# Six dummy products ahead of x's transposition and two behind it, in place of five and one

## The chip, the cores and the metric

The kernel runs on one core of a Trainium2 chip. The metric is device time in microseconds for one launch. A profile is one execution recorded instruction by instruction; its span runs from the first recorded instruction to the last, and the device time of the same execution is somewhat longer.

## The reference

Two blocks read the same x (2048 tokens by 448) and a gate mixes them. Block A is attention with 16 heads of 28 in four segments of 512 tokens, each causal within itself, with a memory carried from segment to segment. Block B is a layer norm and then a two-layer network over the token axis.

```python
x = A_x                                              # (1, 2048, 448), bf16
g = sigmoid((x * gate_w).sum(-1, keepdims=True))
# A: q, k, v = x @ wq, x @ wk, x @ wv; for each segment s of 512 tokens
p = softmax(qs @ ks.T * scale + mask); a_dot = p @ vs
a_mem = (phi(qs) @ M) / (phi(qs) @ z + 1e-6)
o = sigmoid(beta) * a_mem + (1 - sigmoid(beta)) * a_dot
M = M + phi(ks).T @ vs; z = z + phi(ks).sum(0)
a = concat(o) @ wo
# B
u = gelu(einsum('bsd,sf->bdf', layernorm(x), w1) + b1)
b = (einsum('bdf,fs->bds', u, w2) + b2).transpose(0, 2, 1)
return g * a + (1 - g) * b
```

The products that the change touches are no part of this: they multiply a constant by itself, and nobody reads what they write.

## The kernel before

The order of all work is written out by hand in one string, `PLAN` (L30 to L114). An item such as `trx.0.2@P1` names a helper, its arguments, the engine (P for PE, A for ACT, D for DVE, G for POOL, S for SP) and sometimes a bank or buffer number. L1077 walks through the items in order and each helper records one or several operations. Each engine executes its own operations in the order of the string. `Sched.op` (L156) works out from the resources that an operation reads and writes which others it must wait for, and `emit_engine` (L239) puts those waits, as semaphore waits, ahead of the instruction. Between two PE operations that write the same PSUM bank no wait is made (L187).

At the start the string has, on PE: `warm`, then eight `trx` pieces with two transposes each, then `fill`, then the products `kc` of x with the k weights.

- `warm` (L470, matmuls at L474) issues `NWARM` products of a constant array of ones, 128 rows by 512 columns, into PSUM bank 3. `NWARM` is 5 (L25). It reads nothing that is loaded and waits for nothing but the start of the program.
- `ldx` (L375) loads x; the first two pieces, two tiles of 128 tokens each, go into `x0`, with the DMA itself issued at L361 on SP. `xw` (L540) copies 64 columns on ACT so that the last slice is 128 wide.
- `trx` (L544, matmul at L552) transposes 128x128 pieces of the first 512 tokens on PE, against an identity that POOL makes at L465. It waits for the load of x. The other 1536 tokens come transposed by DMA (`xtd`, L417).
- `ex` (L559) copies the transposed pieces from PSUM to `xTb`, on DVE or ACT through the helper `copy` (DVE at L371, ACT at L369).
- `fill` is the helper `keep` (L480, matmul at L481): one product of the same constants into bank 3.
- `pad` (L573) spreads the loaded weights to 32 columns for each head, on DVE at L371. `kc` (L614, matmul at L618) waits for the copies of `ex` and for the padded k weights. `qf` and `kf` follow at L608, and `l2`, `l` at L627.
- `ldwv` (L392) loads wv, `wvc` (L396) copies half of its last slice on DVE.

Behind this stand the value products (L694, L706), the scores (L838) with exponentials on ACT (L848), the products with the probabilities (L879), and the two large products of the token network (`mm_u` at L994, `mm_y` at L1047). Those parts are the same in both kernels.

Of the kernel before, what the change touches and what calls it, by code (L numbers as in the profile page):

```python
# [21 lines left out]
NO = 3  # L22
NTA = 3
RING = 4096
NWARM = 5  # L25
GELU_BATCHES = ((0, 7), (7, 14))


# [117 lines left out]
class Sched:  # L146
# [9 lines left out]
    def op(self, eng, fn, reads=(), writes=(), name=None, dma=False, group=None, out=False):  # L156
        if dma:
            if group is None:
                self._dma_uid += 1
                evspace = "dma_u%d" % self._dma_uid  # L160
            else:
                evspace = "dmag_" + group
        else:
            evspace = eng
        o = Op(eng, evspace, fn, name, len(self.ops))
        if out:
            self.out_spaces.add(evspace)
        deps = {}

        def need(d):  # L170
            if d is o or (dma and d.evspace == evspace):
                return
            key = d.evspace
            old = deps.get(key)
            if old is None or old.idx < d.idx:
                deps[key] = d

        for r in reads:
            if r.last_write is not None:
                need(r.last_write)  # L180
            if r.psum and eng != "PE":
                for rd in r.reads:
                    if rd.eng != eng and rd.eng != "PE":
                        need(rd)
        for r in writes:
            w = r.last_write
            if w is not None and not (r.psum and eng == "PE" and w.evspace == "PE"):  # L187
                need(w)
            for rd in r.reads:
                if not (r.psum and eng == "PE" and rd.evspace == "PE"):  # L190
                    need(rd)
        o.deps = list(deps.values())
        for d in o.deps:
            d.is_event = True
        if dma:
            o.is_event = True
        for r in reads:
            r.reads.append(o)
        for r in writes:
            r.last_write = o  # L200
            r.reads = []
        self.ops.append(o)
        self.per_eng[eng].append(o)
        return o
# [43 lines left out]
def build_kernel(nc, X, WQ, WK, WV, WO, BETA, W1, B1, W2, B2, GW, OUT):  # L248
    sch = Sched(nc)
    op = sch.op  # L250
# [13 lines left out]
    def R(name, n=None, psum=False):  # L264
        if n is None:
            return Res(name, psum)
        return [Res(f"{name}{i}", psum) for i in range(n)]
# [5 lines left out]
    R_bank = R("psum", 8, psum=True)  # L273

    def bank(b):
        return ps[:, b, :]
# [25 lines left out]
    ones = nc.const_aps.tensor(1.0, [128, 512], BF16)  # L302
# [167 lines left out]
    def warm(eng, u):  # L470
        def fn(e):
            last = None
            for _ in range(NWARM):
                last = e.matmul(bank(3)[:, 0:512], ones[:, 0:128], ones[:, 0:512], start=True, stop=True,  # L474
# [3 lines left out]
        op("PE", fn, reads=[], writes=[R_bank[3]])  # L478

    def keep(eng, u):  # L480
        op("PE", lambda e: e.matmul(bank(3)[:, 0:512], ones[:, 0:128], ones[:, 0:512], start=True, stop=True,  # L481
                                    skip_group_check=True), reads=[], writes=[R_bank[3]])

    def acttab(eng, u):
        op("ACT", lambda e: e.activation(gth[:, 0:1], ones[:, 0:1], ACT.Exp), reads=[], writes=[R_gth[0]])
# [577 lines left out]
    def st(eng, u, T):  # L1063
        i = slot["out", T]
        for c0, n in [(0, D)] if T < NT - 1 else [(0, 224), (224, 224)]:
            dma(eng, out2[T * 128 : T * 128 + 128, c0 : c0 + n], outst[:, i, c0 : c0 + n],
                reads=[R_outst[i] if c0 == 0 else R_out2], final=True)

    emit_op = dict(ldx=ldx, ldwk=ldwk, ldwq=ldwq, ldwv=ldwv, wvc=wvc, ldgw=ldgw, ldsm=ldsm, ldwo=ldwo, xtd=xtd, xtc=xtc, ldr=ldr, dve0=dve0,
                   id=ident_, mz=mz, oz=oz, warm=warm, fill=keep, acttab=acttab, btg=btg, btr=btr, gcp=gcp, b1c=b1c_, b2c=b2c_, tb=tb,  # L1070
                   bet=bet, xw=xw, trx=trx, ex=ex, pad=pad, rid=rid, kc=kc, kf=kf, qf=qf, l=l, l2=l2, l3=l3, gw=gw, gr=gr,
                   ek=ek, eq=eq, vf=vf, vl=vl, vl2=vl2, ev=ev, gt=gt, gc=gc, pkm=pkm, pke=pke, pkn=pkn, pqm=pqm,
# [61 lines left out]
```

## Time and profile before

| | before |
|---|---|
| four runs | 175.59, 176.68, 176.68, 177.79 us |
| median | 176.68 us |
| the profiled execution: device time | 175.59 us |
| the profiled execution: span | 173.8 us |
| PE busy | 167.3 us in 1286 matmuls |
| dummies of L474 | 5, starting at 0.82 us, 631 ns each in the median |
| dummy of L481 | 1, starting at 4.72 us, 380 ns |
| transposes of L552 | 16, starting at 3.48 us, 226 ns each in the median |

A line of the timeline gives the start in us, the time from the first start to the last end, engine, line, operation, what is written and read with the shapes, and how many; in brackets the idle time ahead of it and what ended it. [...]matmuls overlap: the rate is read from the distance between two starts, not from the duration. In the table by stretches a row gives the stretch, its length, PE's busy time with the number of matmuls, the clock granted as the records have it, the share of the DMA engines, and GB/s. A line of the chain of waits gives a start, a length and the work or the transfer that the end waited for. The profiled execution is the lowest of the four runs; it lies 1.09 us below the median.

### The profile page before, as it was taken

What the parts mean: (1) busy time and instruction counts of PE and PEld (TensorE: products, weight loads), DVE (VectorE), ACT (ScalarE), POOL (GpSimd) and SP (SyncE); (2) the same over time, 40 slices, a digit from 0 to 9 for tenths busy, and PEclk for the clock granted to TensorE, in tenths of its full rate; (3) what the DMA queues carried; (4) which work ended last, traced back from release to release, by engine and by line L of the source; (5) the groups of instructions that cost most, each with busy time, mean ns of one, the idle gap of its engine ahead of it and who ended that gap; (6) DMA issues with size and microseconds to landing.
All of it is one profiled execution on the core that took longest, in us unless ns stands there. A gap on an engine that the chain in (4) does not pass through costs nothing.

```text
span 173.8 us, 3285 instructions
## 1 busy us (share of the span) xinstructions
PE 167.3 (96%) x1286; PEld 78.6 (45%) x1302; DVE 133.4 (77%) x276; ACT 121.1 (70%) x113; POOL 54.3 (31%) x100
## 2 busy tenths in 40 slices
PE   7799999999999999999999999999999999999994
PEld 3324334344534445444454446444444444455563
DVE  4789999868667875899599486899999879995113
ACT  4229899797969788878997979986697774600300
POOL 7045437880083055412200019033108242200000
PEclk9999999999999999999999999999999999999999
DMA  4897999335940495199690623500727268291022
GB/s 128 264 194 151 279 340 196 63 65 123 301 111 6 55 264 73 25 247 235 180 241 6 178 65 90 155 0 20 215 63 209 83 185 222 68 260 34 0 70 62
DMA packets 49456, 24.01 MB, mean 138 GB/s; under 512 B 14337, under 2 KB 49441, under 8 KB 49441
## 3 DMA queue, kind: packets, MB, share of 16 engines
q1 hardware_dynamic: 49441, 23.81, 55.3%
q8 instruction: 10, 0.16, 0.4%
q14 instruction: 5, 0.04, 0.1%
HBM read 18.48 MB, written 2.18 MB: 119 GB/s over the span
## 4 chain that ended last, share of the span: by engine, by line
PE 83%; DVE 9%; SPq 3%; DMA 2%; issue 1%
PE t L994 25%; PE t L1047 24%; PE t L608 7%; PE t L1020 7%; PE t L838 7%; PE t L879 5%; PE t L694 3%; DVE t L371 3%; SPq L361 3%; DMA t<-in_A_wv_dram 2%; PE t L627 2%; PE t L803 2%; DVE t L948 1%; PE t L706 1%; DVE t L1005 1%
## 5 line engine op out<-in xcount | busy, mean ns | idle before, releaser
L848 ACT ACTIVATE t<-t 128x2048 bf16<-128x2048 f32 x40 | 75.1, 1878 | 20.4 <-PE t L838 19.6
L861 POOL TENSOR_SCALAR_AFFINE_SELECT t<-t 128x1024 bf16<-128x1024 bf16 (+1 forms) x40 | 37.4, 954 | 82.2 <-ACT t L848 82.2
L994 PE MATMUL t<-t 128*128 128x448 bf16 x224 | 49.0, 353 | 0.3 <-issue 0.2
L1047 PE MATMUL t<-t 128*128 128x448 bf16 (+1 forms) x238 | 47.3, 342 | 0.2 <-issue 0.2
L1047 PEld LDWEIGHTS t<-t 128*128 128x128 bf16 x238 | 22.1, 98 | 19.5 <-issue 2.8
L994 PEld LDWEIGHTS t<-t 128*128 128x128 bf16 x224 | 20.9, 98 | 21.5 <-issue 2.5
L371 DVE CAST t<-t 128x512 bf16<-128x512 f32 (+1 forms) x23 | 15.3, 669 | 6.7 <-PE t L608 4.5
L369 ACT ACTIVATE t<-t 128x512 bf16<-128x512 f32 (+5 forms) x28 | 13.9, 533 | 8.8 <-PE t L627 6.1
L1056 DVE SCALAR_TENSOR_TENSOR t<-t 128x448 bf16<-128x448 f32 (+1 forms) x17 | 10.8, 648 | 11.3 <-PE t L1047 11.2
L608 PE MATMUL t<-t 128*128 128x512 bf16 x68 | 18.0, 381 | 0.7 <-issue 0.2
L838 PE MATMUL t<-t 28*128 28x512 bf16 (+3 forms) x256 | 15.9, 301 | 0.1
L1030 ACT ACTIVATE t<-t 128x448 bf16<-128x448 f32 x9 | 6.3, 722 | 12.0 <-PE t L1020 12.0
L1020 PE MATMUL t<-t 128*128 128x448 bf16 x64 | 14.2, 353 | 0.1
L1005 DVE TENSOR_SCALAR t<-t 128x448 bf16<-128x448 f32 x12 | 8.2, 682 | 5.8 <-PE t L994 5.7
L757 ACT ACTIVATE t<-t 128x1024 bf16<-128x1024 bf16 x12 | 12.6, 1050 | 0.0
L899 DVE STREAM_TRANSPOSE t<-t 128x512 f32<-128x512 f32 x16 | 11.1, 697 | 1.3 <-PE t L879 1.3
L940 DVE STREAM_TRANSPOSE t<-t 128x512 bf16<-128x512 bf16 x16 | 10.8, 687 | 0.1
L920 DVE SCALAR_TENSOR_TENSOR t<-t 128x448 bf16<-128x448 f32 x16 | 10.7, 686 | 0.1
L838 PEld LDWEIGHTS t<-t 28*128 28x128 bf16 x256 | 4.5, 92 | 13.9 <-issue 7.1
L694 PE MATMUL t<-t 128*128 128x449 bf16 x48 | 10.7, 355 | 0.0
L879 PE MATMUL t<-t 128*32 128x512 bf16 (+3 forms) x256 | 10.3, 301 | 0.0
L608 PEld LDWEIGHTS t<-t 128*128 128x128 bf16 x75 | 6.3, 97 | 8.5 <-issue 2.9
(77 smaller groups left out, 158.2 us busy)
## 6 DMA issues: line engine op xcount, KB each, us to landing
t<-in_B_w_dram SPq DMA_DIRECT2D x7, 1024.0 KB, 7.6
t<-in_B_w_dram SPq DMA_DIRECT2D x8, 896.0 KB, 5.4
out_dram<-t SPq DMA_DIRECT2D x15, 112.0 KB, 1.8
t<-in_A_x_dram SPq DMA_DIRECT2D x3, 448.0 KB, 7.0
t<-in_A_x_dram SPq DMA_DIRECT2D x2, 224.0 KB, 2.7
t<-in_A_wo_dram SPq DMA_DIRECT2D x4, 98.0 KB
t<-in_A_wk_dram SPq DMA_DIRECT2D x3, 112.0 KB, 3.3
t<-in_A_wq_dram SPq DMA_DIRECT2D x1, 336.0 KB, 3.5
```

The source lines that it names most:

```text
L369: op("ACT", lambda e: e.activation(out, in_, ACT.Copy), reads=reads, writes=writes)
L371: op(eng, lambda e: e.tensor_copy(out, in_), reads=reads, writes=writes)
L608: m = e.matmul(bank(b)[:, 0:512], wkq[:, c0 + c, 128 * hg : 128 * hg + 128], xTb[:, tc % NXT, c, :], start=first and c == 0, stop=last and ...
L694: m = e.matmul(bank(b)[:, 0 : D + 1], xTb[:, tc % NXT, c, k0 : k0 + 128], wvx[:, c, 0 : D + 1], start=tc == 0 and c == 0, stop=tc > 0 and ...
L757: op("ACT", lambda e: e.activation(et[:, i, :].rearrange("p (g t) -> p g t", g=2), two(T, hp, s), ACT.Exp), reads=[RT[2 * hp][s], RT[2 * h ...
L838: last = e.matmul(bank(hl)[:, c0 : c0 + w], kT[r, hg, s * 512 + j * 128 : s * 512 + j * 128 + 128], qT[r, hg, s * 512 + 128 * j : s * 512 ...
L848: op("ACT", lambda e: e.activation(punit(i).rearrange("p (a q) -> p a q", a=4), ps[:, 0:4, :], ACT.Exp, scale=SCALE), reads=R_bank[0:4], w ...
L861: op("POOL", lambda e: e.affine_select(d, d, pattern=pat, compare_op=ALU.is_ge, fill=0.0, base=0, channel_multiplier=-1), reads=[R_P[i]], ...
L879: last = e.matmul(bank(b)[32 * hl : 32 * hl + 32, 128 * j : 512], vaug[:, 4 * s + j, 32 * h : 32 * h + 32], p4[:, hl, c0 : c0 + w], start= ...
L994: op("PE", lambda e: e.matmul(bank(b)[:, 0:D], w[:, st, (ft % 2) * 128 : (ft % 2) * 128 + 128], xtile(st)[:, 0, :], start=(st == 0), stop= ...
L1020: last = e.matmul(bank(b)[:, 0:D], oT[:, hg, T * 128 : T * 128 + 128], wo_sb[:, hg, :], start=(hg == 0), stop=(hg == NHG - 1), skip_group_ ...
L1047: op("PE", lambda e, b=b, f=f, c0=c0, n=n: e.matmul(bank(b)[:, 0:n], w[:, f, c : c + 128], uT[:, f, c0 : c0 + n], start=(f == 0), stop=(f ...
```

## The change

The first group of dummies gets one more product, the later one gets a loop with a count of its own, set to 2. Operands, bank and order stay as they are.

```diff
-NWARM = 5
+NWARM = 6
+NFILL = 2
...
     def keep(eng, u):
-        op("PE", lambda e: e.matmul(bank(3)[:, 0:512], ones[:, 0:128], ones[:, 0:512], start=True, stop=True,
-                                    skip_group_check=True), reads=[], writes=[R_bank[3]])
+        def fn(e):
+            last = None
+            for _ in range(NFILL):
+                last = e.matmul(bank(3)[:, 0:512], ones[:, 0:128], ones[:, 0:512], start=True, stop=True,
+                                skip_group_check=True)
+            return last
+
+        op("PE", fn, reads=[], writes=[R_bank[3]])
```

## The prediction

> **What bounds the kernel now.** I read the page first, for the engine that fills the span, then the chain of waits, then the first ten microseconds, since the edit sits there.
>
> ```profile
> span 173.8 us, 3285 instructions
> ...
> PE 167.3 (96%) x1286; PEld 78.6 (45%) x1302; DVE 133.4 (77%) x276; ACT 121.1 (70%) x113; POOL 54.3 (31%) x100
> ...
> PEclk9999999999999999999999999999999999999999
> ...
> PE 83%; DVE 9%; SPq 3%; DMA 2%; issue 1%
> ```
>
> PE is busy for 96% of the span and carries 83% of the chain that ended last: what delays PE's stream in a stage without slack is paid at the end. The clock row is 9 in every slice, the first too; it says nothing of a slow start, so that has to be read from the spacing of the matmuls. The timeline of PE alone, and busy time in stretches that I cut at its events (the count takes in matmuls that straddle an edge):
>
> ```profile
> 0.82 2.29 PE L474 MATMUL t<-const-bfloat16-1.0 128*128 128x512 bf16 x5 [0.82 <-PEq L1119]
> 3.48 1.40 PE L552 MATMUL t<-t 128*128 128x128 bf16 x16 [0.37 <-DMA t<-in_A_x_dram]
> 4.72 0.38 PE L481 MATMUL t<-const-bfloat16-1.0 128*128 128x512 bf16 x1
> ```
> ```profile
> 2.95:3.48 0.53, 0.16 (x1) 1.00 1.07 370
> ...
> 5.10:5.99 0.89, 0.00 (x0) 1.00 1.00 342
> 5.99:10.06 4.07, 4.06 (x18) 1.00 0.97 217
> ```
>
> Record by record, the dummies of L474 start at 0.82, 1.20, 1.63, 2.05 and 2.48: 427 ns apart after the first. The first transposes of L552 are 107 ns apart; between 4.10 and 4.27 the step falls to 56 ns and stays there. The 18 products from 5.99 to 10.06 are 216 ns apart. So in this execution PE ran at half rate until about 4.22, 3.40 us after its first dummy. PE then stood still from about 5.1 to 5.99 for DVE's padding of the k weights. The chain of waits in the same stretch:
>
> ```profile
> 5.61 4.04 DMA t<-in_A_wv_dram
> ...
> 9.67 0.27 DVE t L371
> 9.95 0.23 DVE t L371
> 10.23 0.61 PE t L627 x4
> ```
>
> The chain does not run through PE before 10.23: it is SP issuing loads, the landing of wv, and two copies on DVE, for which PE waits 0.18 us after its 18 products. That 0.18 us is all the slack PE has there; beyond it, lateness goes into the chain.
>
> [...]
>
> **The change part by part.** The order of instructions differs on PE alone: 5 to 6 in the first group, 1 to 2 in the later one. No wait, DMA or buffer moves; bank 3 is written by PE before and after, so no semaphore is added.
>
> *Sixth dummy, its own cost.* It would start at 2.48 + 0.43 = 2.91 and stream until 3.33. x is there at 3.48, so 0.15 us of cover remain. Its record would end at 2.91 + 0.63 = 3.54, 0.06 past the first transpose, but dummies overlap by 0.20 (631 ns long, 427 apart), so I take 0, with 0.06 as upper end. Were x to land earlier than 3.33 the delay is bounded by 0.43. Queued behind it on PE: all 16 transposes, for which ACT and DVE wait.
>
> *Second product behind the transposes.* It starts at 4.72 + 0.22 = 4.93 and is over by 5.31; the next PE work starts at 5.99, released by DVE. Cover 0.68, cost 0. With PE still at half rate: the 16 transposes would end at 3.48 + 16 x 0.107 = 5.19, and two dummies at 5.19 + 2 x 0.427 = 6.05, up to 0.06 late plus the tail of a record, 0.2: 0 to 0.26, of which 0.18 is slack.
>
> *What the products do to the clock.* This does not appear as an edit, so I bound it. Between 0.82 and 4.22 the dummies streamed 5 x 0.427 = 2.13 us, 63% of 3.40; with the transposes (0.74) 84%. With six: 2.56 us, 75%, or 97%. [...] In an execution where 4.22 was missed, what is lost? [...] Each microsecond of cold PE after 5.99 costs (0.427 - 0.216)/0.427 = 0.49.
>
> That is the size of the scatter of the runs shown: 175.59, 176.68, 176.68, 177.79, steps of 1.1 on three values. The profiled execution (span 173.8, 1.8 around it) is the lowest, 1.09 under the median. If late clocks make the scatter, +1.09 is a change to full clock at 5.99 + (1.09 + 0.18)/0.49 = 8.6, +2.20 one at 10.8. No trace of such an execution is at hand: this is a reading, not a finding. In the profiled execution itself the gain is nothing, its clock being up before it matters.
>
> **Sum.** Against the profiled execution: 0 + 0 + 0.06 at most. Against the median: the ramp comes in time more often, -1.09, bounds -1.5 to 0, and a loss only through the covers named. Likeliest case: the median falls to the level of the profiled execution, 175.59 + 0.06, about **175.7**.
>
> **The rivals.**
>
> *Nothing changes* (176.7). [...] the scatter may come from the landing of wv or from the coarse steps of the timing. For it: the chain before 10.23 is DMA and DVE. Against: 0.18 us of slack is little, and PE is the bound ever after. Chance 0.28.
>
> *Slower: the dummies are themselves in the way* (177.2; 178.8 at worst). Place: PE's queue ahead of the first transpose and of the first k product. Decided when x lands before 3.33 or PE is cold at 5.19. Price 0.43 + 0.26 - 0.18 = 0.5 on the median, 177.2[...]. Against: covers of 0.15 and 0.68 us. Chance 0.16, of which 0.10 beyond 1%.
>
> *Faster than the profiled execution* (174.5). Eight cold transposes would go warm, 8 x 51 ns = 0.41, if the full clock came before 3.48, and DVE's first copy of the transposed x, released by PE at 4.47, would start earlier. Against: the chain then lies in wv's landing, and 0.4 shows up as 174.5 only by the 1.1 steps. Chance 0.12.
>
> That the products would not be issued, or be made one, is excluded by the order of instructions.
>
> **How the numbers follow.** Likeliest case 0.44, the rivals 0.28, 0.16, 0.12. A difference under 1% (1.8 us) is about what a measurement of this kernel can't tell from none. The likeliest case is by itself a gain of 0.6%; it exceeds 1% where the kernel before, timed beside it, stands at its 177.8 end, for which I give 0.18 of the 0.44. Faster: 0.18 + 0.12 = 0.30. Same: 0.26 + 0.28 + 0.06 = 0.60. Slower: 0.10. The range, 174.4 to 177.3, takes in the fast rival, the no-change case and the nearer slow one; it leaves out the 0.10 beyond 1%, and some 0.07 at the edges.
>
> **What would show it.** Right: six L474 records 427 ns apart, the first transpose still released by x's DMA at about 3.5, two records of the later dummy ending before DVE lets the first k product go at about 6.0, and 216 ns spacing from there on; a span of about 173.8, the whole gain lying in how often that span is met, so a narrower scatter. Wrong: a first transpose held by PE's own queue, k products 427 ns apart after 6.0, a span under 173.4, or the same three values with the same frequency.

## The result, and the profile after

| | before | after |
|---|---|---|
| runs beside each other | 56 | 35 |
| median | 176.96 us | 176.82 us |
| lowest and highest | 175.59, 178.22 | 176.04, 178.06 |
| profiled execution, span | 173.8 us | 175.0 us |

The ratio of after to before is 0.9996, 95% interval [0.9982, 1.0009]: no difference larger than 0.2%. The forecast was 175.7; the time lies in its range, but the gain of 0.6% did not come. The profiled execution of after is even 1.2 us longer than that of before, so the two profiles have to be read for what happens to differ between two executions, too.

The page of after, the same lines as before:

```profile
span 175.0 us, 3289 instructions
...
PE 167.7 (96%) x1288; PEld 78.6 (45%) x1304; DVE 133.1 (76%) x276; ACT 121.2 (69%) x113; POOL 54.1 (31%) x100
...
PE 80%; DVE 11%; SPq 4%; DMA 2%; issue 1%
```

Two matmuls more by count, PE busy 0.4 us longer, and 3% of the chain has gone from PE to DVE and SP. The timeline of PE in the opening of after (lines ahead of `keep` lie one further down than before, those behind it seven):

```profile
0.82 2.72 PE L475 MATMUL t<-const-bfloat16-1.0 128*128 128x512 bf16 x6 [0.82 <-PEq L1126]
...
3.60 1.25 PE L559 MATMUL t<-t 128*128 128x128 bf16 x16
4.68 0.60 PE L485 MATMUL t<-const-bfloat16-1.0 128*128 128x512 bf16 x2
5.90 2.77 PE L625 MATMUL t<-t 128*128 128x512 bf16 x12 [0.62 <-ACT t L370]
8.50 1.46 PE L615 MATMUL t<-t 128*128 128x512 bf16 x6
9.89 0.61 PE L634 MATMUL t<-t 64*128 64x512 bf16 x4
```

The sixth dummy ends at 3.54, the transposes begin at 3.60, the second product ends at 5.28, the k products begin at 5.90. The first transposes start at 3.60, 3.66 and 3.72, 67 and 55 ns apart where those of before are 107 apart until 4.20: PE was at its full rate by then, some 0.6 us earlier than in the profile of before. The last-slice products at L634 (L627 before) start at 9.89, 0.34 earlier than before. Only 0.09 of that is PE's own (its last k product starts at 9.58, before at 9.67). The rest comes from the load of wv, which lands at 9.21 here and at 9.64 before, and which the edit does not touch. The lead is gone at once. The chain of waits in after:

```profile
8.88 3.60 DMA t<-in_A_x_dram
12.47 0.02 issue
12.50 0.29 DVE t L372
```

The transposed second quarter of x lands at 12.47, DVE stands still for 0.53 us until then, and from there all is 0.2 us later than before. The other 1 us comes at 69 us, in code that neither edit touches. These are the waits of PE between 66 and 75 us in after (waiting, then released by whom, us in total, times, longest), and the stretches around it with PE, PEld, DVE, ACT and POOL busy, clock, DMA share and GB/s:

```profile
PE t L810 <- DVE t L1012: 0.9, 1, 0.9
PE t L1001 <- DVE t L827: 0.2, 1, 0.2
```
```profile
67.50:69.00 1.50, 1.50 (x15) 0.51 (x12) 1.50 (x3) 0.83 (x1) 0.60 (x1) 1.00 0.01 0
69.00:69.85 0.85, 0.00 (x0) 0.00 (x0) 0.68 (x2) 0.80 (x1) 0.03 (x1) 1.00 0.00 0
69.85:70.90 1.05, 1.00 (x20) 0.92 (x20) 0.00 (x0) 1.05 (x1) 0.00 (x0) 1.00 0.10 14
```

And the same place in the profile of before:

```profile
67.50:68.80 1.30, 1.30 (x16) 0.49 (x14) 1.30 (x4) 0.63 (x1) 0.61 (x1) 1.00 0.00 0
68.80:69.80 1.00, 1.00 (x20) 0.90 (x24) 0.67 (x2) 0.95 (x1) 0.03 (x1) 1.00 0.00 0
```

In after PE does nothing from 69.00 to 69.85, with no data moving. What it waits for is the second product of the memory (`mst.1`, L803 before, L810 after). The line names DVE at L1012, but this writes the token network's tile, which `mst.1` does not read and which stands behind it in the string. `mst` reads four pieces that DMA transposes (`pkt`). In both traces the landing of each of the four is told by 16 semaphore events. Of the last piece's, fifteen come at 68.01 to 68.12 in after, and the sixteenth at 69.70. In before all 16 come from 67.31 to 67.58, and `mst.1` follows at about 68.7 without a wait. That the transfer is what PE waits for is shown by the distance: in all ten profiles in which PE waits at `mst.1`, its first product starts 0.20 us after the sixteenth event, while the DVE line that is named differs from one to the next.

### The profile page after: what moved, and what is told of

It reads as the page before. It is cut to its first block, busy times and chain, and to the rows that moved or that the text cites. A ratio compares the mean times of both kernels' runs of the same rounds, so it can differ in the third digit from the quotient of the medians.

```text
span 175.0 us, 3289 instructions
## 1 busy us (share of the span) xinstructions
PE 167.7 (96%) x1288; PEld 78.6 (45%) x1304; DVE 133.1 (76%) x276; ACT 121.2 (69%) x113; POOL 54.1 (31%) x100
## 4 chain that ended last, share of the span: by engine, by line
PE 80%; DVE 11%; SPq 4%; DMA 2%; issue 1%
PE t L1054 24%; PE t L1001 24%; PE t L1027 7%; PE t L615 7%; PE t L845 6%; SPq L362 4%; PE t L886 4%; PE t L701 3%; DVE t L372 3%; DMA t<-in_A_x_dram 2%; PE t L810 2%; PE t L634 1%; DVE t L955 1%; DVE t L1012 1%; PE t L713 1%
## 5 line engine op out<-in xcount | busy, mean ns | idle before, releaser
L1063 DVE SCALAR_TENSOR_TENSOR t<-t 128x448 bf16<-128x448 f32 (+1 forms) x17 | 10.8, 648 | 11.3 <-PE t L1054 11.2
L1012 DVE TENSOR_SCALAR t<-t 128x448 bf16<-128x448 f32 x12 | 8.2, 682 | 6.6 <-PE t L1001 6.5
```

## The experiments

Theory A: both kernels reach full clock early enough in the median execution, and what separates the runs lies elsewhere. Theory B, that of the prediction: the median of before is 1.1 us above its profiled execution because its clock comes late. Theory C: the opening is set by loads and DVE, whatever the clock. Two more came up on the way. Theory S: most of the scatter is the late last piece at `mst.1`. Theory D: the slowest runs are those with a late clock, and the change makes these rarer, but the median run is in time.

Each kernel was run beside the kernel before, whose medians were 176.98 (42 runs, for e1 to e4), 176.87 (71, e5 to e8) and 176.92 (67, e9 to e12). The ratio is estimated from the single runs and is not the quotient of the two medians; for e8, whose runs form two groups, that quotient would be 1.004. Below, e5, e7, e8 and e11 are shown as diffs against before, e12 against e6, and the others against after.

| kernel | ahead, behind | median (runs) | ratio to before, 95% interval |
|---|---|---|---|
| e1_one_dummy | 1, 0 | 178.27 (7) | 1.0075 [1.0039, 1.0111] |
| e7_three_one | 3, 1 | 177.28 (20) | 1.0027 [1.0004, 1.0051] |
| e8_five_none | 5, 0 | 177.57 (20) | 1.0007 [0.9976, 1.0039] |
| e3_five_two | 5, 2 | 176.94 (20) | 0.9998 [0.9976, 1.0020] |
| e2_six_one | 6, 1 | 176.70 (12) | 0.9970 [0.9942, 0.9997] |
| e10_six_one_again | 6, 1 | 176.72 (14) | 0.9977 [0.9954, 1.0000] |
| e9_six_two_again | 6, 2 | 176.75 (22) | 0.9994 [0.9975, 1.0012] |
| e4_fourteen | 14, 2 | 178.23 (12) | 1.0071 [1.0046, 1.0096] |
| e11_transposes_only | 19 transposes, 1 | 177.38 (20) | 1.0006 [0.9986, 1.0026] |
| e5_state_late_51 | 5, 1, `mst.1` later | 176.39 (20) | 0.9980 [0.9958, 1.0002] |
| e6_state_late_62 | 6, 2, `mst.1` later | 176.40 (20) | 0.9973 [0.9951, 0.9996] |
| e12_fill_then_state | 6, 2, `mst.1` later, filled | 176.12 (20) | 0.9961 [0.9940, 0.9982] |

To see where a profile loses its time I compared the starts of the same ACT instruction with the profile of before. The table gives the shifts in us, near 11.2, 23.4, 66.3 and 79.6 of that profile, and the instant at which the clock is released to full rate. That instant is the first clock record of the trace; after, e7 and e6 hold no such record, and there it is read from the distances between the starts of PE's matmuls (e11's first matmul starts at 1.41, the others' at 0.82):

| kernel | release | 11.2 | 23.4 | 66.3 | 79.6 |
|---|---|---|---|---|---|
| before | 4.2 | 0 | 0 | 0 | 0 |
| after | by 3.6 | -0.34 | +0.21 | +0.20 | +1.16 |
| e2 (6, 1) | 5.8 | -0.15 | -0.14 | +0.18 | +1.07 |
| e10 (6, 1) | 5.1 | +0.16 | +0.17 | +0.28 | +1.17 |
| e9 (6, 2) | 6.6 | +0.32 | +0.33 | +0.46 | +1.49 |
| e3 (5, 2) | 5.5 | -0.11 | -0.10 | +0.90 | +1.79 |
| e7 (3, 1) | 7.4 | +0.51 | +0.56 | +0.56 | +1.45 |
| e5 (5, 1, later) | 9.6 | +1.60 | +1.45 | +1.45 | +1.80 |
| e8 (5, 0) | 9.7 | +1.64 | +1.45 | +1.45 | +2.34 |
| e1 (1, 0) | 10.2 | +1.89 | +1.72 | +1.71 | +2.80 |
| e4 (14, 2) | 3.5 | +1.09 | +0.89 | +0.89 | +1.78 |
| e6 (6, 2, later) | 6.4 | +0.36 | +0.37 | +0.37 | +0.72 |
| e12 (6, 2, filled) | 4.0 | +0.02 | +0.08 | +0.29 | +0.62 |
| e11 (transposes) | 6.6 | +0.09 | +0.10 | +1.05 | +1.94 |

### One dummy and none

```diff
-NWARM = 6
+NWARM = 1
...
-trx.1.3@P fill@P ex.0.1@D
+trx.1.3@P ex.0.1@D
```

> One product ahead of the transposes, none behind. Theory A (before and after both reach full clock early enough, and what scatters the time is something late in the kernel, so the last dummies bought nothing): [...] the k products from about 6 us on are 427 ns apart, [...] DVE's chain waits for them, and the median rises by 0.5 to 2: about 178.2. Theory B (the scatter of the kernel before is already that of a late clock): its median holds 1.1 us of it, so taking dummies away adds at most 1, and its low end near 175.6 is no longer met: about 177.4, all runs above 176.5. Theory C (the opening is set by loads and DVE whatever PE's clock): 176.9, k products at half rate but no later end of DVE's chain.

178.27, as theory A has it; all seven runs between 177.68 and 178.93. PE's timeline, opening:

```profile
3.56 1.89 PE L559 MATMUL t<-t 128*128 128x128 bf16 x16 [2.15 <-DMA t<-in_A_x_dram]
6.16 4.73 PE L625 MATMUL t<-t 128*128 128x512 bf16 x12 [0.71 <-DVE t L372]
```

Twelve k products take 4.73 us where after takes 2.77: they start 427 ns apart until about 10.2. ACT is 1.89 late at 11.2 and still 1.71 late at 66: theory C is out where the clock is late, for the delay goes through to the end. The dummies of before are worth 1.3 us (178.27 - 176.98).

### The halves of the change, alone

```diff
 NWARM = 6
-NFILL = 2
+NFILL = 1
```

> The sixth dummy alone. Theory A: 176.8 to 177.0, no difference; the release of the clock may lie at another time, and what it moves before 10 us is gone by 20 us. Theory B: 0.3 to 0.5 lower than before if the sixth dummy is what brings the clock in time. Rival that the two halves cancel (the sixth dummy holds up the transposes, the second product helps): 0.2 to 0.4 higher than before.

```diff
-NWARM = 6
+NWARM = 5
 NFILL = 2
```

> The second product behind the transposes alone. Theory A: 176.8 to 177.0, the product ends before DVE lets the first k product go, near 6.0. Cancelling halves: 0.2 to 0.4 lower than before.

176.70 and 176.94. No cancelling: neither is slower than before. Six and one is the better by 0.2 to 0.3%, at the edge of its interval (and again in its second batch, below). In both profiles the release (at 5.8 and 5.5 us) lies behind all transposes and ahead of the first k product; up to 23.4 us both are 0.1 us ahead of before, and at 79.6 they are 1.07 and 1.79 behind. What they lose they lose later, at `mst.1` and in a place ahead of it. The layer norm needs the last tiles of x that are loaded as they are, not transposed, and in these executions DVE has to wait for them. Chain of waits in e2, then DVE's timeline in e3:

```profile
18.48 7.46 DMA t<-in_A_x_dram
25.94 0.02 issue
25.96 1.17 DVE t L955 x2
```
```profile
26.68 1.15 DVE L955 BATCH_NORM_STATS2 t<-t 128x6 f32<-128x448 bf16 x2 [1.10 <-DMA t<-in_A_x_dram]
```

In before that load lands at 25.74, in e2 at 25.94, in e3 at 26.66. Between 23.4 and 66.3 us e2 loses 0.32 and e3 1.00 (there PE also waits 0.7 for the last transposed quarter of x); e9, e10 and e12 lose 0.11 to 0.21 there and e11 0.95. The profiles that are 0.5 us late or more at 23.4 lose nothing there.

### Fourteen dummies

```diff
-NWARM = 6
+NWARM = 14
```

> Fourteen dummies ahead, two behind: the dummies now run past the landing of x. With the clock up at about 4.2 they end at 0.82 + 8 x 0.427 + 6 x 0.216 = 5.5, so the first transpose is 2.0 us late and held by PE's own queue. Theory A: DVE's idle of 1.1 us before the q weights and 0.4 before wv take up most of it, the rest shows: 177.5 to 178.3. Theory C: 176.9, all of it absorbed. Theory B: no gain over six, as the clock is up anyway: 177.5 to 178.3 too.

178.23, the upper end of theory A and B. PE's timeline shows the first transpose at 5.17, held by PE itself with x long landed:

```profile
0.82 4.51 PE L475 MATMUL t<-const-bfloat16-1.0 128*128 128x512 bf16 x14 [0.82 <-PEq L1126]
5.17 1.05 PE L559 MATMUL t<-t 128*128 128x128 bf16 x16
```

It is 1.7 us later than in before; 1.09 of that is left at 11.2 and 0.89 at 66. So the cover ahead of the transposes is small, and beyond it about half of what the dummies delay is still there in this profile. The profiled execution, at 177.36, is the second lowest of the twelve; the median is 0.87 above it, and no profile shows a median execution of e4.

### The memory product behind other work

`mst.1`, its readers, and one DVE item (`ta.4`) move within the hand-written order; the two versions differ in the dummies only.

```diff
-sc.3.1@P mst.1@P2 eu.6@D exp.3.1@A3 gw.2@S pv.4@P12 msa.1@D pv.5@P31 msc.1@D mask.3.1@G
-sc.3.2@P mem.6@P22 ta.4@D exp.3.2@A4 u.5.11@P u.5.12@P u.5.13@P ot.0@D
+sc.3.1@P eu.6@D exp.3.1@A3 gw.2@S pv.4@P12 ta.4@D pv.5@P31 mst.1@P2 msa.1@D msc.1@D mask.3.1@G
+sc.3.2@P exp.3.2@A4 u.5.11@P u.5.12@P u.5.13@P mem.6@P22 ot.0@D
```

> The dummies as before (five and one); the second memory product, which waits for four DMA transposes near 69 us, is put behind the two probability products that followed it (1.2 us of PE work), with its reader 0.6 us later. Theory S (the scatter of the kernel before is mostly the late last part of one DMA transpose there, 0.9 to 1.2 us in most executions and absent in the one profiled first): the median falls by 0.6 to 1.0, to about 176.1, and the profile shows no idle PE before the product. Theory B (the scatter is a late clock): 176.9, nothing won. Rival that the moved product is itself in the way (its reader waits for the copy): 177.0 to 177.5.

> The same move with six dummies and two. Theory S, with dummies that no longer matter: equal to the five-and-one version with that move within 0.3, about 176.1. Theory that a gain of the dummies was hidden behind that wait: 0.3 to 0.5 below it.

176.39 and 176.40: 0.5 us under the kernel before, with the dummies of before and of after alike. That is theory S's direction, but less than the 0.6 to 1.0 that it expected (the interval of 0.998 takes in 1, that of 0.9973 does not). PE no longer stands still at `mst.1`; timeline of PE in e6:

```profile
69.40 1.32 PE L886 MATMUL t<-t 128*32 128x512 bf16 x32 [0.23 <-DVE t L372]
70.65 1.07 PE L810 MATMUL t<-t 128*128 128x128 bf16 x16
71.65 0.40 PE L845 MATMUL t<-t 28*128 28x256 bf16 x8
```

The sixteenth event of the last piece came at 69.60 here, 1.58 us behind the fifteenth, as in after; it is covered now, and both profiles lose 0.35 between 66 and 80 us where after loses 0.96. So about half of the 1.1 us between the profiled execution of before and its median went away with the move, with either set of dummies; it is nothing that the dummies can reach.

The profile of e5 gave what I had not been able to look at before: an opening that is instruction for instruction that of before, in an execution whose clock is late. PE's busy time with the number of matmuls in two stretches from the first k product:

```profile
6.14:9.55 3.41, 3.41 (x9) 1.00 0.89 206
9.55:11.74 2.19, 2.19 (x11) 1.00 0.89 179
```

Nine matmuls in 3.41 us, then eleven in 2.19: half rate up to 9.6. The column of the granted clock says 1.00 in both. It costs 1.60 at 11.2 and 1.45 from 23 us on. So the late clock is real. But this execution, at 177.36, is the eighteenth of the 20 runs in order of time, not the median one.

The two versions also differ in their slower runs. With `mst.1` behind other work, 8 of 20 runs of e5 lie above 176.8, apart from the rest, and 3 of 20 runs of e6.

### Three dummies, and five with none behind

```diff
-NWARM = 5
+NWARM = 3
```

> Three dummies ahead, one behind. Theory A [...]: three give 1.28 us before the transposes, [...] some k products at 427 ns; median 177.0 to 177.7, between the kernel before and the one without dummies (178.3). If any dummy at all sufficed: 176.9, and k products at 216 from the first.

```diff
-trx.1.3@P fill@P ex.0.1@D
+trx.1.3@P ex.0.1@D
```

> Five dummies ahead, none behind. Theory A: full clock by about 6 from the five alone, 176.9 to 177.1. If the single product behind the transposes is what keeps the clock coming: 177.3 or more, and a release after 6.0 in the profile.

Three and one: 177.28, as expected, with the clock up at 7.4. Five and none: a median of 177.57 that hides two groups. Nine runs lie from 176.04 to 176.85, ten from 177.71 to 178.53, one between. The profile is of the upper group, with the clock at 9.7, which is not the 176.9 to 177.1 of theory A but the other side of what was expected. With two groups of about the same size the interval of 0.9976 to 1.0039 is wide and takes in 1; the count says more, 10 of 20 runs in the upper group against 16 of 71 of the kernel before. The one product behind the transposes seems to be worth more than its place in PE's idle time would tell.

### How often the clock is late

The runs of before have the same two groups: in the first batch 11 of 56 lie above 177.5, in the others 12 of 42, 16 of 71 and 16 of 67. Of these 236 runs only one lies between 177.5 and 177.75, at 177.58; the 54 above have a median of 177.9, the rest one of 176.8. So the changed kernel (e9, the same as after) and its first half (e10, the same as e2) were run again.

> The changed kernel once more, with more executions. Runs of the kernel before fall into two groups with nothing between 177.5 and 177.8; 39 of 169 lie above. Theory D (the upper group is the executions in which the clock is released near 9.7 us and not by 6.4; the changed kernel's extra products make these rarer, but the median execution of both kernels is on time): above 177.5 under 12 in 100 of this kernel's runs against some 23 of the kernel before, medians within 0.2. Rival (the dummies do not bear on the groups): the same share as in the kernel before.

> Six ahead, one behind, once more (0 of 12 runs were above 177.5). Theory D: under 12 in 100 above 177.5, median 176.6 to 176.9. If the 12 were luck: 23 in 100, and a median of 176.9.

Of six and two, 2 of 22 lie above 177.5 (before beside it: 16 of 67), and 4 of 35 in its first batch (11 of 56). Of six and one, 1 of 14, after 0 of 12. That is theory D's side: 7 of 83 with six dummies. Four of the seven lie at 177.53 to 177.63, below the upper group of before; above 177.7 there are 3 of 83, against 54 of 236. The medians are within 0.2 of before, as it said. No single one of these batches is decisive, the line at 177.7 was drawn after the runs were seen, and a share is not a release: that a run of the upper group has a late clock is shown by the profiles of e5 and e8 alone. No profile of before itself shows one, nor an execution at its median.

### Transposes in place of the dummies

```diff
-                last = e.matmul(bank(3)[:, 0:512], ones[:, 0:128], ones[:, 0:512], start=True, stop=True,
-                                skip_group_check=True)
+                last = e.matmul(bank(3).bitcast(BF16)[:, 0:128], ident[:, :], ident[:, :], is_transpose=True,
+                                start=True, stop=True, skip_group_check=True)
...
-        op("PE", fn, reads=[], writes=[R_bank[3]])
+        op("PE", fn, reads=[R_ident], writes=[R_bank[3]])
```

`NWARM` is 19, and the identity is recorded ahead of it.

> The five dummy products are replaced by 19 dummy transposes of the identity, 2.0 us of PE work at half rate from 1.4 us on, when the identity is there; the one product behind x's transposes stays. [...] release by 7 at the latest, as with five products, median 176.7 to 177.1. [...] as without dummies, release at 7.5 to 10.3 and a median near 178.

177.38, between the two forecasts; the highest of 20 runs is 177.64, the group near 178 is missing. The release in its profile, near 6.6, lies where the first forecast put it, by 7: 3.6 us sooner than in e1, which has one product of the constants ahead of 6 us as e11 has. That is one execution of each. The release cost it little: the profiled execution, at 177.49 near the median, is only 0.09 late at 11.2. It loses 0.95 between 23.4 and 66.3, where DVE waits 1.10 us for tiles of x, and 0.89 at `mst.1`. Why these loads come later in e11 stays open.

### Two products of the token network ahead of it as well

```diff
-sc.3.1@P eu.6@D exp.3.1@A3 gw.2@S pv.4@P12
+sc.3.1@P u.5.11@P u.5.12@P eu.6@D exp.3.1@A3 gw.2@S pv.4@P12
...
-exp.3.2@A4 u.5.11@P u.5.12@P u.5.13@P mem.6@P22 ot.0@D u.5.14@P
+exp.3.2@A4 u.5.13@P ot.0@D u.5.14@P mem.6@P22
```

> Six and two, with the second memory product behind the probability products as in the version before, and two products of the token network ahead of these, so that their mask is ready. Theory S (what is left of the stall there is 0.35 us): 0.1 to 0.3 under the version without the two, so 176.1 to 176.3, a ratio of about 0.996. Rival: the exponentials start 0.4 later and PE waits for them instead: 176.4 to 176.9.

176.12, ratio 0.9961 [0.9940, 0.9982]: the lowest median of all, 0.6 us under that of e9, the changed kernel in the same batch; 17 of its 20 runs lie below 176.4, of e9's 22 one. PE's timeline has no wait left there:

```profile
69.03 0.55 PE L1001 MATMUL t<-t 128*128 128x448 bf16 x2
69.51 1.27 PE L886 MATMUL t<-t 128*32 128x512 bf16 x32
70.71 1.07 PE L810 MATMUL t<-t 128*128 128x128 bf16 x16
```

Its profile still loses 0.33 between 66 and 80 us, as those of e5 and e6 do, so the reason given ahead of the run, a remaining stall of 0.35 us, is not what it removed; where the 0.3 us against e6 come from is not shown. The gain over after lies in the order of the work around `mst.1`; the dummies are those of after.

## Why the prediction was wrong

*What bounds the kernel*: right. PE's lateness in the opening goes through to the end (e1: 1.71 of 1.89 us are left at 66 us), and the slack in front of the last-slice products is small. What it did not have are the barriers behind. An early PE runs into a load: in after x's second quarter lands at 12.47 and takes the lead of 0.34, in e2 and e3 the last tiles of x for the layer norm take theirs near 26 us.

*Own cost of the dummies*: right for both. In after the transposes follow at 3.60, and the second product is over 0.62 us before the k products begin. That there is a limit is shown by e4: nine dummies more ahead than in before, and one behind, raise the median by 1.25 us. In e9, whose transposes started early, at 3.38, nothing was lost that the median shows.

*Price of a late clock*: right in size. The 0.49 us for each microsecond of cold PE after 5.99 gives (9.6 - 6.14) x 0.49 - 0.18 = 1.5 for e5; measured 1.60 at 11.2 and 1.45 afterwards. With one dummy the clock came at 10.2 and the median rose by 1.3. The instant of a late release was an estimate of mine, 8.6, worked out from the 1.09 between the profile and the median; in e5, with the same opening, it came at 9.61.

*The sum*: this is the step that failed. It said that "the ramp comes in time more often, -1.09", and that the likeliest case is that "the median falls to the level of the profiled execution". It rests on the sentence "If late clocks make the scatter, +1.09 is a change to full clock at 5.99 + (1.09 + 0.18)/0.49 = 8.6". So the whole distance between one profile and the median was put down to the clock. In place of it the runs showed two causes.

The first sets the median. The ten other profiles with `mst.1` in its old place lose 0.89 to 1.09 us between 66 and 80 us, late clock or not. Two of them, after (176.71) and e10 (176.72), are executions near their own medians and within 0.3 us of that of before, and their clock is up by 3.6 and at 5.1. Moving `mst.1` lowers the median by 0.5 with either set of dummies. The profile that the prediction argued from was a rare one: of 236 runs of before 13 lie under 175.95. That the median execution of before is in time and waits at `mst.1` is the reading that fits all this; no profile of that execution exists, and the move won 0.5 of the 1.1 us.

The second is the late clock. It belongs to the upper group, about one run of before in four or five, 1.1 us above the rest. With the change this group shrinks, from 16 in 67 to 2 in 22 and from 11 in 56 to 4 in 35. A tenth of the runs by 1.1 us is 0.1 us in the mean (177.05 to 176.95 in the first batch, 177.01 to 176.82 in the second) and next to nothing in the median: the ramp does seem to come in time more often, and the median hardly moves.

The first rival, that nothing changes, held (176.7 against 176.82), and in part for its reasons. In after, e2, e3, e6, e10, e11 and e12, whose clock is up by 6.6 us, wv lands between 9.21 and 10.00, and the shift at 11.2 is the distance of that landing from the 9.64 of before to within 0.1. (In e9 a part of x landed 0.8 us later than in before, at 4.77, and the shift comes from there.) So the landing of wv does scatter the opening by some 0.4 us to either side; it does not make the steps of 1.1. The slower rival, dummies in the way, did not come at 6 and 2 but is what e4 shows; its 178.8 at worst was an estimate of mine. The steps of 1.1 us on three values, in which I saw late clocks, were four runs; 56 fill the gaps up to 177.5.

## What to carry to other kernels

A median moves only if the median execution has the fault: before an edit is priced by the distance between a profile and the median, look at several profiles, or at how the runs are grouped, and find out which executions have it. A profiled execution that is the fastest of its runs is a poor base, since what it lacks can't be read from it. The dummy products (PE reached its full rate at 4.2 in the profile with five and one, at 10.2 in that with one) were free here only up to the arrival of the data that the next products wait for (fourteen cost 1.25 us), and an earlier PE was worth nothing where the next stage waited for a transfer.

## What the runs showed of the hardware

The clock column reads 1.00 at both rates: in e5 nine matmuls took 3.41 us with 1.00 beside them, and the next eleven 2.19 us with 1.00 again. The trace of before holds no clock record ahead of 4.21, and that of after none for the whole span. In before, e5 and e1 the first record stands at 4.21, 9.61 and 10.19, within 0.1 us of the instant at which the distance between starts changes from 427 ns to 216 ns for 512 columns (e5, e1), or from 107 ns to 56 ns for a transpose (before).

The release came at different places with the same opening: five and one had it at 4.21 (before) and 9.61 (e5), six and two by 3.6 (after), at 4.0 (e12), 6.4 (e6) and 6.6 (e9). What decides between them was not shown.

The straggling event at `mst.1` came at nearly the same distance wherever it came: in 11 of 14 profiles the sixteenth event came 1.58 us, give or take 0.02, after the fifteenth. In the same 11 a transfer of 16 KB on the instruction queue (q8) had ended 1.18 us before it (after: 68.53 and 69.70; e1: 70.16 and 71.34; e12: 68.39 and 69.57). In e4 and e11, where that transfer ended 1.9 and 2.1 us before the first event, there was no straggler; there all sixteen events came late, from 69.83 and 70.21 on, and PE lost 0.89 all the same. In before the transfer ran from 66.75 to 67.83, from 0.56 ahead of the first event of the piece to 0.52 behind it, as in after (0.58 and 0.52), and no event was more than 0.14 behind the one ahead of it. No run moved that transfer, and the cause of the straggler was not shown.
